# First group's third unit in seven products on summed factors, with three steps of ScalarE at other places

## The chip, the cores and the metric

The kernel runs on one core of one Trainium2 chip. The metric is device time in microseconds (us) of one execution; lower is better. TensorE (PE in the profile) multiplies matrices and writes to eight PSUM banks; VectorE (DVE) and ScalarE (ACT) do elementwise work and empty the banks; GpSimd (POOL) and SyncE (SP) here mostly issue DMAs. Each engine works through its own queue in order, and semaphores tie the queues together.

## The reference

A causal linear attention with decay, then a feed-forward layer:

```
for each block of 64 positions:                      # B=4, H=8, S=768, D=64
    intra = ((q_b @ k_b.T) * Dmask) @ v_b
    inter = (q_b * lam_pow) @ kv_state
    out   = intra + inter
    kv_state = lam_block * kv_state + (k_b * rev_pow).T @ v_b
x = out as (3072 tokens, 512)
h = x @ w_in                                         # 512 x 2048
g = h - tanh(h)
result = g @ w_out                                   # 2048 x 512
```

q, k, v and lam are float32. w_in and w_out come as 64-bit floats and are rounded to float32 on the chip.

## The kernel before, in words

**Groups and units.** The tokens are worked in NG = 6 groups of 512 (128 positions of each of 4 sequences). The 2048 columns of w_in are NU = 4 units of 512. A unit of h for one group is a 512 x 512 result, kept as a 2 x 2 grid of 256 x 256 corners named 11, 21, 12 and 22. A corner of h sits in one PSUM bank and goes through tanh (ScalarE) and a subtraction (VectorE) into the tiles g11, g21, g12, g22 (`hidden`, line 545).

**Two ways to a unit.** `up_plain` (line 953) computes a corner as a plain sum over four blocks of 128: 8 matmuls for each of 4 corners, 32 for a unit. `up` (line 540) computes one of seven products of Winograd's form of Strassen's scheme: sums of weight quarters (`ws`, made by `sums_in`, line 257) times sums of token quarters (`tt` and T3, made by `att_sums`, line 509), 4 matmuls for a product, 28 for a unit. Products are collected in three banks y, z and w: ScalarE copies y into w after product 1, so that product 2 adds to it; copies of y after products 6 and 7 and additions of z on VectorE give the other corners. `sums_in` overwrites the quarter a21 of the unit's weights with the sum S3, so that plain corners can't be computed from it any more. Before, group 0 uses `up_plain` for all its units; group 1 uses `up` for all.

**The stage in question** is group 0's: the weights of w_in are rounded while it computes (`round_block`, line 281: three ScalarE steps at lines 291 to 293 and two VectorE steps at 295 and 296 for each of 16 blocks of w_in and then 16 of w_out). Units 1 to 3 are done corner by corner, and between the corners lie pieces of the attention of group 1: `att_transpose`, `att_scores`, `att_state`, `att_inter`, `att_intra`, for sequences 0 and 1 (p0) and then 2 and 3 (p1). The list `turns` (line 1058) sets this order: unit, corner, how many blocks of w_out to round, attention pieces. Then follows the loop over kt (line 1080): `down_first` (line 984) multiplies 128 rows of g at a time with seven products, all seven accumulated in seven banks over kt = 0 to 7; `sums_out` (line 264) makes the weight sums of one kt and stores them to DRAM for later groups; kt = 2 and 5 keep their two blocks in `ws` tiles that are not yet used (`pair_tiles`, line 249). `sums_first` (line 979) makes S1 = g12 + g22 and g12 = g11 - g12 for one unit; `sums_late` the rest.

**Order.** The planner of the tile framework orders the instructions of each engine by the order in which they are written and by when it expects their inputs; what is ready may be pulled far forward. `tied(yes, op)` (line 125) keeps an instruction in the written order among the others that are tied on its engine. Between `att_inter` and `att_intra` (four banks left open) `held["yes"]` is true; `att_inter` ends in a small ScalarE read, `seen` (line 486), which the intra matmuls wait for. `att_state` (line 413) scales the old state on ScalarE (line 431); `powers` (line 108) fills `mask` on ScalarE and `fwd` on VectorE, both needed by group 1's attention. GI = 2 is the first group of the later, more finely split form.

Of the kernel before, what the change touches and what calls it, by code (L numbers as in the profile page):

```python
# [16 lines left out]
AL = mybir.AluOpType  # L17
# [7 lines left out]
def kernel(  # L25
# [223 lines left out]
    def pair_tiles(kt):  # L249

        if kt % 3 == 2:
            return tuple(ws[u].rearrange("p x k c -> p (x k) c")[:, 0:4] for u in (3, 2))
        wt = wst.tile([128, 8, 256], F32, name="wt", tag="w")
        return wt[:, 0:4], wt[:, 4:8]

# [156 lines left out]
    def att_state(g, bs):  # L412
        pair_ = slice(bs[0], bs[0] + 2)
        if g == 0:
            kv = bank("kv", "att", 4).rearrange("d (b p e) -> d b p e", b=2, p=NP)
            for n, b in enumerate(bs):
                kd, vn = raw[g, b]["k"], raw[g, b]["v"]
                for p in range(NP):
                    for j in range(2):
                        tc.keep_in_program_order(nc.tensor.matmul(  # L420
                            out=kv[ts(j, 64), n, p, :], lhsT=kd[:, 2 * p + j, :], rhs=vn[:, 2 * p + j, :],
                            start=n == 0 and p == 0, stop=True, skip_group_check=True))
            tc.keep_in_program_order(nc.scalar.activation(states(1)[0][:, pair_], kv, AF.Copy))
            return


        old, mid, new = (x[:, pair_] for x in states(g))
        subs = (0, 1) if g < NG - 1 else (0,)
        kv = [bank("kv", "att", 4).rearrange("d (b p e) -> d b p e", b=2, p=NP) for _ in subs]
        for p in range(NP):  # L430
            nc.scalar.activation(mid[:, :, p], old[:, :, p], AF.Copy, scale=fwd[:, p, HALF - 1:HALF])
        for n, b in enumerate(bs):
            kd, vn = raw[g, b]["k"], raw[g, b]["v"]
            for p in range(NP):
                for j in range(2):
                    for a in subs:
                        tied(g != GI, nc.tensor.matmul(
                            out=kv[a][ts(j, 64), n, p, :], lhsT=kd[ts(a, 64), 2 * p + j, :],
                            rhs=vn[ts(a, 64), 2 * p + j, :], start=n == 0 and p == 0, stop=True,
                            skip_group_check=True))  # L440
        nc.vector.tensor_tensor(mid, mid, kv[0], op=AL.add)
        for p in range(NP) if g < NG - 1 else ():
            nc.vector.scalar_tensor_tensor(out=new[:, :, p], in0=mid[:, :, p], scalar=fwd[:, p, HALF - 1:HALF],
                                           in1=kv[1][:, :, p], op0=AL.mult, op1=AL.add)
# [64 lines left out]
    def att_sums(g, bs):  # L509
        x0, x1 = xt[g, 0], xt[g, 1]  # L510
        b11, b21, b12, b22 = x0[:, 0:2], x0[:, 2:4], x1[:, 0:2], x1[:, 2:4]
        tt = xpool.tile([128, 3, 2, HB], F32, name="tt", tag="tt")
        nc.vector.tensor_tensor(tt[:, 0], b12, b11, op=AL.subtract)
        nc.vector.tensor_tensor(tt[:, 1], b22, tt[:, 0], op=AL.subtract)
        nc.vector.tensor_tensor(b12, b22, b12, op=AL.subtract)
        nc.vector.tensor_tensor(tt[:, 2], b21, tt[:, 1], op=AL.subtract)
        xt[g] = dict(B11=b11, B21=b21, B22=b22, T1=tt[:, 0], T2=tt[:, 1], T3=b12, T4=tt[:, 2])
# [27 lines left out]
    def up(g, u, n):  # L545
        a, bname = FACT[n]
        wt = {"A11": w1[u][:, 0:2, 0], "A12": w1[u][:, 2:4, 0], "S3": w1[u][:, 0:2, 1], "A22": w1[u][:, 2:4, 1],
              "S1": ws[u][:, 0], "S2": ws[u][:, 1], "S4": ws[u][:, 2]}[a]
        x = xt[g][bname] if bname != "B11" else xt[g, 0][:, 0:2]
        key = ("up", g, u)  # L550
        t, first = product_bank(key, n)
        for m in range(2):
            for kt in range(2):
                nc.tensor.matmul(out=t[:, m, :], lhsT=wt[:, kt, ts(m, 128)], rhs=x[:, kt, :],  # L554
                                 start=first and m == 0 and kt == 0, stop=kt == 1, skip_group_check=True)

        def dst(c):
            return hidden(g, c)[:, u]

        def finish(c, src):  # L560
            th = work.tile([128, 2, HB], F32, name="th", tag="th")
            nc.scalar.activation(th, src, AF.Tanh)
            nc.vector.tensor_tensor(dst(c), src, th, op=AL.subtract)

        y, z, w = (banks[key, x].rearrange("q (m c) -> q m c", m=2) if (key, x) in banks else None for x in "yzw")
        if n == 1:
            w = banks[key, "w"] = bank("w", "w", 1)
            nc.scalar.activation(w, banks[key, "y"], AF.Copy)
        elif n == 2:
            finish(11, w)  # L570
        elif n == 6:
            nc.scalar.activation(dst(12), y, AF.Copy)
        elif n == 7:
            nc.scalar.activation(dst(22), y, AF.Copy)
            nc.vector.tensor_tensor(dst(22), dst(22), z, op=AL.add)
            finish(22, dst(22))
        elif n == 4:
            finish(21, y)
        elif n == 3:
            nc.vector.tensor_tensor(dst(12), dst(12), z, op=AL.add)  # L580
# [355 lines left out]
    def every(steps):  # L936
        for _ in steps:
            pass
# [15 lines left out]
    def up_plain(u, cs):  # L954

        hm = {}
        for c in cs:
            a, t = divmod(c - 11, 10)
            hm[c] = bank("h", ("ya", "yb", "z", "w")[2 * t + a], 1).rearrange("q (m c) -> q m c", m=2)
        for i in range(KI):  # L960
            for c in cs:
                a, t = divmod(c - 11, 10)
                for m in range(2):
                    tied(u == 0 or held["yes"], nc.tensor.matmul(  # L964
                        out=hm[c][:, m, :], lhsT=w1[u][:, i, a, ts(m, 128)], rhs=xt[0, t][:, i, :],
                        start=m == 0 and i == 0, stop=i == KI - 1, skip_group_check=True))
                if (i, c) != (KI - 1, cs[-1]):
                    yield
        for c in cs:
            th = work.tile([128, 2, HB], F32, name="th", tag="th")  # L970
            nc.scalar.activation(th, hm[c], AF.Tanh)
            nc.vector.tensor_tensor(hidden(0, c)[:, u], hm[c], th, op=AL.subtract)  # L972
        yield
# [4 lines left out]

    def sums_first(u):
        g11, g12, g22, s1 = (hidden(0, c)[:, u] for c in (11, 12, 22, "S1"))  # L980
        nc.vector.tensor_tensor(s1, g12, g22, op=AL.add)
        nc.vector.tensor_tensor(g12, g11, g12, op=AL.subtract)

    def down_first(kt, ns):

# [39 lines left out]
    for b in (0, 1):  # L1025
# [29 lines left out]
    every(up_plain(0, (12, 22)))  # L1055
    sums_first(0)
    p0, p1 = attention(1)
    turns = [(1, 11, 2, ()), (1, 21, 2, ()), (1, 12, 2, ()), (1, 22, 2, ()), (2, 11, 0, ()), (2, 21, 1, p0[0:1]),
             (3, 11, 0, p0[1:3]), (3, 21, 1, p0[3:4]), (2, 12, 1, p0[4:]), (2, 22, 1, p1[0:1]), (3, 12, 1, p1[1:3]),
             (3, 22, 1, ())]  # L1060
    for u, c, n, more in turns:
        every(up_plain(u, (c,)))
        ahead = (u, c) == (2, 12)
        if ahead:
            run(more)
        weights(ready["done"] + n, u > 1)
        if not ahead:
            run(more)
        if c == 22:
            sums_first(u)  # L1070
            if u == 1:
                ready["to"] = len(blocks)
                load(B + 2)
                load_weights(NU * KI + 2)
                load(B + 3)
                load_weights(NU * KI + WAHEAD)
                load(2 * B)
                powers()
    sums_out(0)
    weights(NU * KI + 6, True)  # L1080
    for kt in range(KH):
        down_first(kt, (1, 2))
        if kt == 0:
            run(p1[3:4])
            down_first(kt, (5,))
            run(p1[4:])
        if kt + 1 < KH:
            sums_out(kt + 1)
        sums_late(kt)
        down_first(kt, (4, 7, 6, 3) if kt == 0 else (5, 4, 7, 6, 3) if kt + 1 < KH else (5, 6, 7, 4, 3))  # L1090
        if kt + 3 < KH:
            weights(ready["done"] + 2)
        if kt in (1, 4, 6):
            sums_in((1, 4, 6).index(kt))
    first_results()
    early.close()
    late["blk"] = ctx.enter_context(tc.tile_pool(name="blk", bufs=2 * B - 1))
# [174 lines left out]
```

## Time and profile before

| | us |
|---|---|
| three timed runs | 650.4, 649.97, 647.11 |
| their median | 649.97 |
| the profiled execution | 646.58 |
| its span | 644.8 |
| TensorE busy in the span | 635.1 |
| VectorE | 478.2 |
| ScalarE | 268.0 |

The span runs from the first to the last instruction of the program; the profiled execution's own time is 1.8 us more. TensorE's time as 'busy' counts each instruction from its start to a modelled end, and these overlap, so the step from one start to the next tells more than the length of one. A line of a timeline has the start, the length of a run of like instructions, the engine, the line of the kernel, what it writes and reads, the count, and the idle time of the engine before it with what released it.

### The profile page before, as it was taken

To read this page: it belongs to the slowest core of one execution; us is meant where nothing else is said; L and a number is where in the kernel's file an instruction comes from. 1 tells how busy PE (TensorE), PEld (TensorE's weight loads), DVE (VectorE), ACT (ScalarE), POOL (GpSimd) and SP (SyncE) were. 2 spreads that over 40 slices of the span, in tenths; PEclk is the share of its full clock that TensorE was granted. 3 is DMA by queue.
4 is the path that set the end of the run, shared out by engine and by line. 5 is a ranking of instruction groups with operands and counts; after the bars stand their busy time and mean duration, and the time that the engine had idled before them with its cause. 6 is when DMAs were issued, how large, how long until landed. Compare 5 with 4: busy or idle time off the path is not lost.

```text
span 644.8 us, 16628 instructions
## 1 busy us (share of the span) xinstructions
PE 635.1 (98%) x6440; PEld 583.6 (91%) x6440; DVE 478.2 (74%) x948; ACT 268.0 (42%) x620; POOL 229.0 (36%) x397
## 2 busy tenths in 40 slices
PE   8899999999999999999999999999999999999998
PEld 6788878888888999998999998999998899998997
DVE  4577597785888877579968579987668987467953
ACT  3799576503432422345331337233245332334310
POOL 0000355735443454411455430355321254521261
PEclk9999999999999999999999999999999999999999
DMA  9999988969765999884889976798883477732384
GB/s 216 233 244 232 294 265 268 348 187 267 210 164 126 288 278 298 224 188 112 230 236 304 280 203 157 184 276 249 253 198 80 138 234 241 248 105 77 100 296 145
DMA packets 166190, 139.80 MB, mean 217 GB/s; under 512 B 136864, under 2 KB 138016, under 8 KB 166112
## 3 DMA queue, kind: packets, MB, share of 16 engines
q0 software_dynamic: 31792, 104.62, 50.0%
q1 hardware_dynamic: 134176, 34.12, 25.9%
q8 instruction: 51, 0.84, 0.5%
q14 instruction: 27, 0.22, 0.1%
q10 hardware_dynamic: 144, 0.00, 0.0%
HBM read 111.94 MB, written 26.74 MB: 215 GB/s over the span
## 4 chain that ended last, share of the span: by engine, by line
PE 65%; issue 18%; POOL 8%; DVE 3%; DMA 3%; ACT 2%; SPq 2%; POOLq 0%; DVEq 0%
PE plain L849 10%; PE acc L993 7%; PE h L964 7%; PE y L906 6%; PE y L697 6%; PE zw L906 4%; PE y L554 4%; POOL wb L795 4%; PE z L697 3%; PE zs L619 2%; PE z L554 2%; PE y L619 2%; POOL wb L792 2%; PE op L501 1%; PE w L697 1%
## 5 line engine op out<-in xcount | busy, mean ns | idle before, releaser
L795 POOL DMA_DIRECT2D wb<-fine x133 | 71.8, 541 | 157.5 <-PE plain L849 107.8
L849 PE MATMUL plain<-wb,g 128*128 128x256 f32 x416 | 96.0, 381 | 0.0
L849 PEld LDWEIGHTS plain<-wb,g 128*128 128x128 f32 x416 | 77.5, 190 | 10.4
L964 PE MATMUL h<-xt,w 128*128 128x256 f32 x256 | 57.9, 382 | 1.8 <-DVE w L296 1.8
L798 POOL DMA_DIRECT2D wb<-factors x64 | 34.6, 541 | 69.2 <-PE z L697 47.9
L910 ACT ACTIVATE q<-y 128x128 f32<-128x128 f32 x76 | 21.1, 278 | 86.1 <-PE y L906 85.0
L964 PEld LDWEIGHTS h<-xt,w 128*128 128x128 f32 x256 | 47.7, 190 | 9.0 <-DVE w L296 2.0
L906 PE MATMUL y<-wb,g 128*128 128x128 f32 x336 | 44.8, 278 | 0.0
L792 POOL DMA_DIRECT2D wb<-fine_in x60 | 32.6, 545 | 29.3 <-PE z L697 11.0
L600 ACT ACTIVATE th<-g 128x512 f32<-128x512 f32 x48 | 29.5, 628 | 29.0 <-DVE g L625 28.9
L906 PEld LDWEIGHTS y<-wb,g 128*128 128x128 f32 x336 | 40.7, 192 | 0.7
L688 ACT ACTIVATE g<-y 128x512 f32<-128x512 f32 x24 | 14.3, 597 | 63.1 <-PE y L697 63.1
L404 ACT ACTIVATE k_nat<-k_nat,mask 128x64 f32<-128x64 f32 (+1 forms) x128 | 35.1, 338 | 0.6 <-DMA k_nat<-in_k_dram 0.6
L993 PE MATMUL acc<-wt,g 128*128 128x256 f32 x144 | 32.9, 380 | 0.2 <-DVE g L972 0.2
L601 DVE TENSOR_TENSOR g<-g,th 128x512 f32<-128x512 f32 x48 | 32.2, 687 | 0.4
L697 PE MATMUL z<-tt,wb 128*128 128x128 f32 x256 | 31.9, 275 | 0.0
L993 PEld LDWEIGHTS acc<-wt,g 128*128 128x128 f32 x144 | 27.2, 190 | 4.3 <-DVE g L972 0.6
L619 PE MATMUL y<-xt,w 128*128 128x256 f32 x128 | 30.3, 379 | 0.0
L619 PE MATMUL zs<-xt,ws 128*128 128x256 f32 x128 | 30.2, 379 | 0.0
L906 PE MATMUL zw<-wb,g 128*128 128x128 f32 x224 | 30.2, 278 | 0.0
L697 PEld LDWEIGHTS z<-tt,wb 128*128 128x128 f32 x256 | 30.2, 192 | 0.0
L292 ACT ACTIVATE r<-raw 128x512 int16<-128x512 uint32 x32 | 25.0, 782 | 8.3 <-DMA raw<-in_moe_w_out_dram 3.8
(236 smaller groups left out, 1476.2 us busy)
## 6 DMA issues: line engine op xcount, KB each, us to landing
wb<-fine POOLq DMA_DIRECT2D x133, 256.0 KB, 4.0
wb<-factors POOLq DMA_DIRECT2D x64, 256.0 KB, 4.3
wb<-fine_in POOLq DMA_DIRECT2D x60, 256.0 KB, 4.8
v_nat<-in_v_dram SPq DMA_DIRECT2D x24, 256.0 KB, 5.3
raw<-in_moe_w_out_dram POOLq DMA_DIRECT2D x12, 512.0 KB, 5.7
k_nat<-in_k_dram SPq DMA_DIRECT2D x20, 256.0 KB, 4.6
fine<-wt POOLq DMA_DIRECT2D x17, 256.0 KB, 3.4
raw<-in_moe_w_in_dram SPq DMA_DIRECT2D x8, 512.0 KB, 5.2
```

The costliest lines, as they stand in the source:

```text
L404: tc.keep_in_program_order(nc.scalar.activation(k_h, k_h, AF.Copy, scale=mask[0:rows, h % 2, h // 2, HALF - 1:HALF]))
L554: nc.tensor.matmul(out=t[:, m, :], lhsT=wt[:, kt, ts(m, 128)], rhs=x[:, kt, :], start=first and m == 0 and kt == 0, stop=kt == 1, skip_gro ...
L601: nc.vector.tensor_tensor(dst(c), src, th, op=AL.subtract)
L619: nc.tensor.matmul(out=t[:, m, :], lhsT=wt[:, kt, ts(m, 128)], rhs=x[:, kt, :], start=False, stop=kt == 1, skip_group_check=True)
L697: nc.tensor.matmul(out=dst[:, ts(u, 128)], lhsT=a, rhs=b, start=(x in (1, 5) or x == 2 and not filled) and u == 0, stop=True, skip_group_c ...
L792: nc.gpsimd.dma_start(out=t.rearrange("p m c -> p (m c)"), in_=fine_in[INNER.index(n_[1]), (5, 6, 3).index(x_)].rearrange("p u c -> p (u c)"))
L795: nc.gpsimd.dma_start(out=t.rearrange("p m c -> p (m c)"), in_=fine[TWICE.index(n_), SUB.index(x_)].rearrange("p u c -> p (u c)"))
L798: nc.gpsimd.dma_start(out=t, in_=factors[XAT[FACT[n_][1]]][:, 2 * x_:2 * x_ + 2, :])
L849: tied(held["yes"], nc.tensor.matmul(out=t[:, m, :], lhsT=a[:, u, kt, ts(m, 128)], rhs=wb[:, kt, :], start=first and u == 0 and m == 0 and ...
L906: tied(held["yes"], nc.tensor.matmul(out=dst, lhsT=a[:, u, :], rhs=wb[:, ts(u, 128)], start=x in (1, 2) and u == 0, stop=u == NU - 1, skip ...
L964: tied(u == 0 or held["yes"], nc.tensor.matmul(out=hm[c][:, m, :], lhsT=w1[u][:, i, a, ts(m, 128)], rhs=xt[0, t][:, i, :], start=m == 0 an ...
L993: tied(held["yes"], nc.tensor.matmul(out=acc[n][:, r, :], lhsT=a[:, ts(r, 128)], rhs=b, start=kt == 0 and r == 0, stop=kt == KH - 1, skip_ ...
```

## The change

Unit 2 of group 0 (its third) is computed by the seven products of `up` and no longer by `up_plain`. For this:

- `att_sums(0)` is written after unit 1's first corner. T3 goes into the place of S1 of unit 3, since group 0's B12 is still needed by unit 3's plain corners; `sums_first(3)`, which fills that place, moves to kt = 3.
- `sums_in(2)` moves from kt = 6 to after unit 1's second corner; `sums_in(1)` moves from kt = 4 to kt = 6; kt = 2 and 5 keep a block in `ws[1]` in place of `ws[2]`.
- `sums_first(1)` moves to kt = 0; both late ones are tied.
- unit 3's corners alternate between the banks w and yb.
- `powers` (mask) moves behind product 5 of unit 2.
- the sixth block of w_out is rounded behind the last intra matmuls; it and the two blocks after it are tied in kt = 0.
- the scaling of the state for group 2 is tied.

```diff
     def pair_tiles(kt):
-            return tuple(ws[u].rearrange("p x k c -> p (x k) c")[:, 0:4] for u in (3, 2))
+            return tuple(ws[u].rearrange("p x k c -> p (x k) c")[:, 0:4] for u in (3, 1))
...
         for p in range(NP):
-            nc.scalar.activation(mid[:, :, p], old[:, :, p], AF.Copy, scale=fwd[:, p, HALF - 1:HALF])
+            tied(g == GI, nc.scalar.activation(mid[:, :, p], old[:, :, p], AF.Copy, scale=fwd[:, p, HALF - 1:HALF]))
...
-        nc.vector.tensor_tensor(b12, b22, b12, op=AL.subtract)
+        t3 = b12 if g > 0 else hidden(0, "S1")[:, NU - 1]
+        nc.vector.tensor_tensor(t3, b22, b12, op=AL.subtract)
...
     def up(g, u, n):
-                nc.tensor.matmul(out=t[:, m, :], lhsT=wt[:, kt, ts(m, 128)], rhs=x[:, kt, :],
-                                 start=first and m == 0 and kt == 0, stop=kt == 1, skip_group_check=True)
+                tied(held["yes"], nc.tensor.matmul(
+                    out=t[:, m, :], lhsT=wt[:, kt, ts(m, 128)], rhs=x[:, kt, :], start=first and m == 0 and kt == 0,
+                    stop=kt == 1, skip_group_check=True))
...
     def up_plain(u, cs):
-            hm[c] = bank("h", ("ya", "yb", "z", "w")[2 * t + a], 1).rearrange("q (m c) -> q m c", m=2)
+            tag = ("w", "yb")[a] if u == NU - 1 else ("ya", "yb", "z", "w")[2 * t + a]
+            hm[c] = bank("h", tag, 1).rearrange("q (m c) -> q m c", m=2)
...
     def sums_first(u):
-        nc.vector.tensor_tensor(s1, g12, g22, op=AL.add)
-        nc.vector.tensor_tensor(g12, g11, g12, op=AL.subtract)
+        tied(u > 0, nc.vector.tensor_tensor(s1, g12, g22, op=AL.add))
+        tied(u > 0, nc.vector.tensor_tensor(g12, g11, g12, op=AL.subtract))
...
-    turns = [(1, 11, 2, ()), (1, 21, 2, ()), (1, 12, 2, ()), (1, 22, 2, ()), (2, 11, 0, ()), (2, 21, 1, p0[0:1]),
-             (3, 11, 0, p0[1:3]), (3, 21, 1, p0[3:4]), (2, 12, 1, p0[4:]), (2, 22, 1, p1[0:1]), (3, 12, 1, p1[1:3]),
-             (3, 22, 1, ())]
...
+    for c in (11, 21, 12, 22):
+        every(up_plain(1, (c,)))
+        weights(ready["done"] + 2)
+        if c == 11:
+            att_sums(0, None)
+        if c == 21:
+            sums_in(2)
...
+    turns = [(2, 1, 0, ()), (2, 5, 0, ()), (2, 2, 0, ()), (2, 6, 0, p0[0:1]), (3, 11, 0, p0[1:3]), (2, 7, 1, ()),
+             (3, 21, 0, p0[3:4]), (2, 4, 1, p0[4:]), (3, 12, 1, p1[0:1]), (2, 3, 1, p1[1:3]), (3, 22, 1, ())]
+    for u, x, n, more in turns:
+        if u == 2:
+            up(0, u, x)
+        else:
+            every(up_plain(u, (x,)))
+        ahead = (u, x) == (2, 4)
         if ahead:
             run(more)
-        weights(ready["done"] + n, u > 1)
+        weights(ready["done"] + n, True)
         if not ahead:
             run(more)
...
+        if (u, x) == (2, 5):
+            powers()
     sums_out(0)
-    weights(NU * KI + 6, True)
+    weights(NU * KI + 4, True)
     for kt in range(KH):
         down_first(kt, (1, 2))
         if kt == 0:
             run(p1[3:4])
             down_first(kt, (5,))
             run(p1[4:])
+            weights(NU * KI + 6, True)
...
         if kt + 3 < KH:
-            weights(ready["done"] + 2)
-        if kt in (1, 4, 6):
-            sums_in((1, 4, 6).index(kt))
+            weights(ready["done"] + 2, kt == 0)
+        if kt in (0, 3):
+            sums_first(1 if kt == 0 else NU - 1)
+        if kt in (1, 6):
+            sums_in(kt // 6)
```

More of the change, by code (lines that the diff above doesn't have):

```diff
@@ L514, in att_sums @@
         nc.vector.tensor_tensor(tt[:, 1], b22, tt[:, 0], op=AL.subtract)
-        nc.vector.tensor_tensor(b12, b22, b12, op=AL.subtract)
+        t3 = b12 if g > 0 else hidden(0, "S1")[:, NU - 1]
+        nc.vector.tensor_tensor(t3, b22, b12, op=AL.subtract)
         nc.vector.tensor_tensor(tt[:, 2], b21, tt[:, 1], op=AL.subtract)
-        xt[g] = dict(B11=b11, B21=b21, B22=b22, T1=tt[:, 0], T2=tt[:, 1], T3=b12, T4=tt[:, 2])
+        xt[g] = dict(B11=b11, B21=b21, B22=b22, T1=tt[:, 0], T2=tt[:, 1], T3=t3, T4=tt[:, 2])
     def attention(g):
@@ L1057 @@
     p0, p1 = attention(1)
-    turns = [(1, 11, 2, ()), (1, 21, 2, ()), (1, 12, 2, ()), (1, 22, 2, ()), (2, 11, 0, ()), (2, 21, 1, p0[0:1]),
-             (3, 11, 0, p0[1:3]), (3, 21, 1, p0[3:4]), (2, 12, 1, p0[4:]), (2, 22, 1, p1[0:1]), (3, 12, 1, p1[1:3]),
-             (3, 22, 1, ())]
-    for u, c, n, more in turns:
-        every(up_plain(u, (c,)))
-        ahead = (u, c) == (2, 12)
+    for c in (11, 21, 12, 22):
[5 more added lines that the diff above has]
+            sums_in(2)
+    ready["to"] = len(blocks)
+    load(B + 2)
+    load_weights(NU * KI + 2)
+    load(B + 3)
+    load_weights(NU * KI + WAHEAD)
+    load(2 * B)
+    turns = [(2, 1, 0, ()), (2, 5, 0, ()), (2, 2, 0, ()), (2, 6, 0, p0[0:1]), (3, 11, 0, p0[1:3]), (2, 7, 1, ()),
[6 more added lines that the diff above has]
+        ahead = (u, x) == (2, 4)
         if ahead:
             run(more)
-        weights(ready["done"] + n, u > 1)
+        weights(ready["done"] + n, True)
         if not ahead:
             run(more)
[L1069 to L1078, printed above, removed]
+        if (u, x) == (2, 5):
+            powers()
     sums_out(0)
-    weights(NU * KI + 6, True)
+    weights(NU * KI + 4, True)
     for kt in range(KH):
```

## The prediction

> **What bounds the kernel now.** I read the busy table first, then TensorE's busy time by stretches of 10 us over the first 200 us, then who TensorE waited for, then the timelines of TensorE and ScalarE over the stage that the diff touches (30 to 140 us), and last the timelines behind it.
>
> ```profile
> PE 635.1 (98%) x6440; PEld 583.6 (91%) x6440; DVE 478.2 (74%) x948; ACT 268.0 (42%) x620; POOL 229.0 (36%) x397
> ```
>
> TensorE is busy for 98% of the span, and the granted clock is full in all 40 slices. The list of TensorE's waits for 30 to 200 us has three entries only:
>
> ```profile
> PE op L501 <- ACT seen L486: 0.9, 1, 0.9
> PE h L964 <- DVE w L296: 0.8, 1, 0.8
> PE acc L993 <- DVE g L972: 0.2, 1, 0.2
> ```
>
> The second is the last wait of the start-up, at 30.22 us. So from there on a matmul less is worth its full step, and a new wait costs its full length, unless something later takes it back. The timeline of TensorE (start, length, line, idle time before it with its releaser) gives the step and the two waits:
>
> ```profile
> 30.22 29.62 PE L964 MATMUL h<-xt,w 128*128 128x256 f32 x136 [0.81 <-DVE w L296]
> 59.67 0.60 PE L340 MATMUL tp<-ident,q_nat 128*128 128x128 f32 x4
> ...
> 90.92 1.89 PE L993 MATMUL acc<-wt,g 128*128 128x256 f32 x8
> 93.00 1.13 PE L993 MATMUL acc<-wt,g 128*128 128x256 f32 x4 [0.19 <-DVE g L972]
> 94.06 1.16 PE L482 MATMUL op<-qd,state 64*64 64x64 f32 x64
> 95.15 1.13 PE L993 MATMUL acc<-wt,gS 128*128 128x256 f32 x4
> 97.15 1.16 PE L501 MATMUL op<-ss,v_nat 64*64 64x64 f32 x64 [0.88 <-ACT seen L486]
> ```
>
> 136 instructions take 59.67 - 30.22 = 29.45 us, 0.2165 us each (the 379 ns that the page gives is one instruction's length; they overlap). Each written matmul of this shape is two instructions: a unit has 4 corners x 4 x 2 = 32 matmuls, four units 128, and the page counts 256. The wait at 93.00 costs 93.00 - 90.92 - 8 x 0.2165 = 0.35 us. That at 97.15: 97.15 - 95.15 - 4 x 0.2165 = 1.13, less the 0.19 that the same switch cost in the first half (71.74 + 16 x 0.2165 = 75.20, next start 75.39): 0.94 us. What stood ahead of `seen` in ScalarE's order:
>
> ```profile
> 94.51 0.79 ACT L292 ACTIVATE r<-raw 128x512 int16<-128x512 uint32 x1 [0.95 <-DVE ws L296]
> 95.17 0.76 ACT L293 ACTIVATE r<-raw 128x512 f16<-128x512 f32 x1
> 95.80 1.25 ACT L431 ACTIVATE state<-state,fwd 128x128 f32<-128x128 f32 x4
> 96.95 0.15 ACT L486 ACTIVATE seen<-op 128x4 f32<-128x4 f32 x1
> ```
>
> `seen` reads what the inter matmuls (94.06 to 95.22) leave, and two rounding steps and four scalings of group 2's state (written far later, pulled forward by the planner since they were untied) run before it.
>
> **The change part by part.** Times are of this execution; unit 2 starts at 30.22 + 104 x 0.2165 = 52.74.
>
> *Products for corners.* 28 matmuls for 32 is 8 instructions less: 8 x 0.2165 = **-1.73 us**. [...]
>
> *Added VectorE work.* Group 0's token sums (L513 to L516: 4 of 0.69), two additions of z (2 x 0.685); moved up are unit 2's weight sums (4 x 0.683, from after 134 us to about 47), moved back is unit 1's pair at 54.32 and 55.27. Up to 60 us that is 2.7 + 2.7 - 1.4 = 4.0 us more; the stretches 30 to 60 leave VectorE 3.7 + 1.7 + 2.7 = 8.1 us idle. Unit 2's last block is rounded at 47.06 and S1 is wanted at 52.74 + 8 x 0.2165 = 54.47: 7.4 us of cover. Cost 0; without that cover up to the 4.0 us.
>
> *Added ScalarE work.* Three copies of 0.6 us. The critical one seeds bank w between product 1 (ends 54.47) and product 2 (starts 56.20). Here ScalarE is full:
>
> ```profile
> 53.46 0.67 ACT L291 ACTIVATE w<-raw 128x512 f32<-128x512 f32 x1
> 54.03 0.77 ACT L292 ACTIVATE r<-raw 128x512 int16<-128x512 uint32 x1
> 54.66 0.77 ACT L293 ACTIVATE r<-raw 128x512 f16<-128x512 f32 x1
> 55.29 1.68 ACT L111 ACTIVATE mask<-mask 64x256 f32<-64x256 f32 x4
> 57.00 0.60 ACT L971 ACTIVATE th<-h 128x512 f32<-128x512 f32 x1
> ```
>
> Behind the rounding the copy ends at 55.29 + 0.58 = 55.9 and TensorE loses nothing; behind the mask too, at 57.6, it loses 1.4. The mask is now written behind the copy, so I take 0.2, range 0 to 1.4.
>
> *Banks.* Unit 3's corner 11 wants bank w at 61.42; product 2 leaves it at 57.94, and tanh and subtraction need about 1.5 us (57.00 to 58.32 for another corner). Cover 1.9 us; behind the first six scalings of group 1's state (58.81 to 60.68) 0.6 would be lost. I take 0. Corner 22 of unit 3 moves from w to yb. Down-product 2, the one that waits at 93.00, then finds w long free, and yb is wanted only by product 6, behind two attention pieces: **-0.35**.
>
> *Second half's scores.* Today q and k are copied at 82.56 to 84.6, behind a rounding, and scores start at 85.33, a corner (16 instructions) after the transposes. Now one product (8 instructions) lies between, while as many as before (96) lie ahead of the transposes: scores are wanted at 85.33 - 1.73 = 83.6. Copies at their old place would cost 84.6 - 83.6 = 1.0; directly behind the transposes (4 steps of 0.48 from 80.6, as from 61.06 to 62.49) they are done by 82.7 and cost nothing. I take 0.3, range 0 to 1.0.
>
> *ScalarE ahead of `seen`.* Group 2's scaling is tied to its place in group 1's stage, where ScalarE is 22 to 48% busy (170 to 200 us) and its sum is not wanted before 204.45; the sixth block's rounding is written behind the intra matmuls. Ahead of `seen` remain only earlier blocks, the last of which ended at 87.9. **-0.94**, range 0 to -0.94: TensorE has only product 5 (0.87 us) between the two attention pieces, so one rounding step of 0.78 in the way gives most of it back. What the moves cost: the sixth block now runs from about 99.6 to 101.4 and its four differences end by 103.5, wanted at 108.71. Tied too, the next pair's rounding waits for its tile (102.00 today) and holds unit 1's pair of sums on VectorE to about 106.2, wanted at 108.71. Both free. The raw buffer of the sixth block comes free later, and POOL's queue holds the next raw load and the factor stores behind it; the last pair's differences end at 133.54 and are wanted at 138.93, 5.4 us of cover.
>
> *ws[1] for ws[2]*, and unit 1's weight sums from 129.7 to about 134: wanted after 155. Nothing. SP's loads keep their place.
>
> Sum: -1.73 - 0.35 - 0.94 + 0.2 + 0.3 = **-2.5 us**: the profiled execution's 646.58 (span 644.8) would be 644.1. That execution is faster than all three timed runs (median 649.97, 647.11 to 650.4). So I put the same difference on the median: **647.5**.
>
> **Rivals.**
> 1. *All of it, no new wait, and TensorE's one long wait near the end goes too* (0.59 us at 618.92, on a piece from DRAM): -1.73 - 0.35 - 0.94 - 0.59 = -3.6, 646.4. For it: every new wait has a place in ScalarE's order where it costs nothing. Against: that piece is requested when TensorE frees a buffer, so it should move along.
> 2. *New bank waits eat the gain.* Unit 2 and 3 now share four banks with ScalarE copies in the chain. [...] This change packs more onto w and yb. With the upper ends above, 1.4 + 0.6 + 1.0 = 3.0 against 1.73 + 0.35 + 0.94 = 3.0 saved: 650.0. Against: by the rows only the seed copy has less than a microsecond of cover.
> 3. *ScalarE's order becomes the bound, slower than before.* ScalarE is full from 30 to 55 us, and the planner orders what isn't tied. A block's rounding takes it 1.8 us (from 29.29 to 31.09). One block ahead of the seed copy (cover 0.3), of the second half's copies (0.9) and of `seen` (0.6) costs 1.5 + 0.9 + 1.2 = 3.6, with 1.73 + 0.35 = 2.1 saved, since `seen`'s 0.94 isn't: +1.5. Two blocks ahead of the first two and `seen` as it is: 3.3 + 2.7 - 2.1 = +3.9, 653.9. So it is slower from about one block at two of these places, and by more than 0.5% from two. For it: the copies stood behind a block today. Against: from 60 to 80 us ScalarE is free for 6.7 of 20 us, so a copy that is ready seldom has to queue.
> 4. *The products don't run as written*, because the planner moves untied matmuls: the count below would still fall by 8, so -1.73 stays and only the waits differ. It is part of the forecast's range and gets no chance of its own.
>
> **How the numbers follow.** Forecast 0.55, first rival 0.2, second 0.15, third 0.1. A measurement of this kernel can tell about 0.5% (3.2 us) from no change. The forecast (0.4%) and the second lie within it, the first just beyond, the third beyond on the other side; as the timed runs spread over 3.3 us, a little of the forecast goes beyond too: faster 0.25, same 0.65, slower 0.1. Range: from the profiled execution's level with all known gains, 646.58 - 3.0 = 643.5, to the second rival with some of the spread, 650.5.
>
> **What would show it.** Instructions at the plain corner's line 192 and at the product's line 280 (now 256 and 224). No wait of TensorE for `seen` and none for bank w at the first down-product. The seed copy ahead of the mask. The first down-product starting at 90.92 - 1.73 = 89.2, plus any new wait; group 1's first product at 143.24 - 2.5 = 140.7. I am wrong if TensorE shows a wait of over a microsecond between 52 and 90 us, or if that start moves and the span doesn't.

## The result, and the profile after

The changed kernel takes 650.86 us (median of 20 executions, 648.62 to 652.57), the kernel before 649.45 (20 executions, 646.04 to 652.70): a ratio of 1.0031, 95% interval 1.0017 to 1.0044. Forecast was a fall of 2.5 us; it is a rise, of 1.4 us by the two medians and of 2.0 by the ratio. The profiled execution took 650.84 us with a span of 649.1 (646.58 and 644.8 before).

The first part went as forecast. The page's busy table has eight matmul instructions less, 8 x 0.2165 = 1.73 us:

```profile
PE 636.7 (98%) x6432; PEld 583.6 (90%) x6432; DVE 481.6 (74%) x954; ACT 269.2 (41%) x623; POOL 228.7 (35%) x397
```

The list of TensorE's waits from 30 to 200 us (total, times, longest) has lost `seen` and bank w's `g L972`, and has two new entries:

```profile
PE acc L996 <- DVE g L1004: 3.1, 2, 2.7
PE h L967 <- DVE w L296: 1.2, 1, 1.2
PE sp L362 <- ACT kt L342: 0.3, 1, 0.3
```

TensorE's timeline shows where they stand. Both kernels start this stage at 30.22. The second half's scores wait a little (84.70), the first down-product starts at 89.81 (90.92 before), and the intra matmuls follow without a wait:

```profile
84.70 0.69 PE L362 MATMUL sp<-qt,kt 64*64 64x64 f32 x32 [0.28 <-ACT kt L342]
85.21 1.11 PE L437 MATMUL kv<-v_nat,k_nat 64*64 64x64 f32 x64
86.26 3.72 PE L967 MATMUL h<-xt,w 128*128 128x256 f32 x16
89.81 1.89 PE L996 MATMUL acc<-wt,g 128*128 128x256 f32 x8
...
126.07 1.60 PE L996 MATMUL acc<-wt,g 128*128 128x256 f32 x4 [2.75 <-DVE g L1004]
127.46 3.15 PE L996 MATMUL acc<-ws,g 128*128 128x256 f32 x8
130.45 1.03 PE L996 MATMUL acc<-ws,gS 128*128 128x256 f32 x4
```

kt = 1's product 5 starts at 100.56, against 102.67: 2.11 us gained. Then it is lost: 0.56 us at 104.57 and 2.91 at 126.07 on L1004, the second difference of `sums_late` (L1001 before), and 0.25 at 116.15 on L1003, the first. Behind the longest wait come 8 matmuls at twice their step, 1.7 us more. Group 1's first product starts at 146.85 instead of 143.24, 3.6 us later; behind it this profile loses only 0.7 us more to its end.

VectorE's timeline shows what held L1004 at 126. It is written behind the rounding of kt = 6's two blocks (L295, L296) and `sums_first(3)` (L984), and ran in that order:

```profile
119.04 0.43 DVE L1003 TENSOR_TENSOR g<-gS,g 128x256 f32<-128x256 f32 x1 [1.27 <-PE acc L996]
122.82 1.06 DVE L295 TENSOR_SCALAR wt<-wt 128x512 uint32<-128x512 uint32 x2 [3.35 <-ACT wt L291]
123.80 1.27 DVE L296 CUSTOM_DVE_ANT_0 wt<-wt,r 128x1024 uint16<-128x1024 uint16 x2
125.00 0.68 DVE L984 TENSOR_TENSOR gS<-g,g 128x512 f32<-128x512 f32 x1
125.60 0.41 DVE L1004 TENSOR_TENSOR g<-g,g 128x256 f32<-128x256 f32 x1
```

L1004's own input was there from 119.5 on. The 3.35 us before L295 come from ScalarE, which had a step of another block ahead of it, and that block (number 13, counted from 0) had not landed:

```profile
121.50 0.78 ACT L292 ACTIVATE r<-raw 128x512 int16<-128x512 uint32 x1 [6.58 <-DMA raw<-in_moe_w_out_dram]
122.14 1.22 ACT L291 ACTIVATE wt<-raw 128x512 f32<-128x512 f32 x2
```

It landed at 121.39; before, at 117.41. Its buffer was free at about 107.6, when ScalarE's last step on block 9 ended, but POOL's queue issued the load only at 113.38, behind seven stores of kt = 3's factors:

```profile
107.34 0.54 POOL L216 DMA_DIRECT2D raw<-in_moe_w_out_dram  x1 [1.93 <-ACT wt L291]
107.87 0.55 POOL L272 DMA_DIRECT2D factors<-wt  x1
...
113.38 1.10 POOL L216 DMA_DIRECT2D raw<-in_moe_w_out_dram  x2 [0.78 <-DMA factors<-wt]
```

POOL's timeline of the kernel before:

```profile
108.15 0.55 POOL L216 DMA_DIRECT2D raw<-in_moe_w_out_dram  x1 [0.59 <-ACT wt L291]
...
111.34 1.07 POOL L216 DMA_DIRECT2D raw<-in_moe_w_out_dram  x2
```

There block 13's load left 2.0 us sooner, although its buffer came free later (at 108.4): only four of the seven stores stood between it and block 12's load. The other half of the 4 us is the transfer itself: 8.0 us from issue to landing against 6.1. Why it took longer is not shown.

In the kernel before, L1001 of that kt ran at 121.93, between the two L296, and TensorE waited for nothing:

```profile
120.60 0.41 DVE L1000 TENSOR_TENSOR g<-gS,g 128x256 f32<-128x256 f32 x1
120.93 0.68 DVE L296 CUSTOM_DVE_ANT_0 wt<-wt,r 128x1024 uint16<-128x1024 uint16 x1
121.53 0.48 DVE L295 TENSOR_SCALAR wt<-wt 128x512 uint32<-128x512 uint32 x1
121.93 0.41 DVE L1001 TENSOR_TENSOR g<-g,g 128x256 f32<-128x256 f32 x1
122.26 0.68 DVE L296 CUSTOM_DVE_ANT_0 wt<-wt,r 128x1024 uint16<-128x1024 uint16 x1
```

(Of `tied` it was said that an instruction keeps its place among the tied ones. In these traces it runs right behind the one written just before it on its engine, tied or not: `sums_first(3)` behind block 13's L296 here, and behind kt = 3's L1004 in the first experiment.)

### The profile page after: what moved, and what is told of

The parts are those of the page before. It is cut to its first block, busy times and chain, and to the rows that moved or that the text cites. A ratio compares the mean times of both kernels' runs of the same rounds, so it can differ in the third digit from the quotient of the medians.

```text
span 649.1 us, 16621 instructions
## 1 busy us (share of the span) xinstructions
PE 636.7 (98%) x6432; PEld 583.6 (90%) x6432; DVE 481.6 (74%) x954; ACT 269.2 (41%) x623; POOL 228.7 (35%) x397
## 4 chain that ended last, share of the span: by engine, by line
PE 63%; issue 11%; POOL 5%; DMA 2%; DVE 0%; POOLq 0%
PE plain L851 12%; PE y L699 8%; PE y L908 7%; PE zw L908 5%; PE y L555 4%; PE z L699 4%; PE acc L996 3%; POOL wb L797 3%; PE y L621 3%; PE zs L621 3%; PE z L555 2%; PE w L699 2%; DMA wb<-fine 2%; PE sp L362 1%; PE op L482 1%
## 5 line engine op out<-in xcount | busy, mean ns | idle before, releaser
L967 PE MATMUL h<-xt,w 128*128 128x256 f32 x192 | 43.5, 382 | 1.8 <-DVE w L296 1.7
L967 PEld LDWEIGHTS h<-xt,w 128*128 128x128 f32 x192 | 35.8, 190 | 7.4 <-DVE w L296 2.0
L216 POOL DMA_DIRECT2D raw<-in_moe_w_out_dram x12 | 6.9, 574 | 85.8 <-ACT r L293 83.0
```

The costliest lines, as they stand in the source:

```text
L967: tied(u == 0 or held["yes"], nc.tensor.matmul(out=hm[c][:, m, :], lhsT=w1[u][:, i, a, ts(m, 128)], rhs=xt[0, t][:, i, :], start=m == 0 an ...
```

## The experiments

Ratios are to the kernel before in the same series, by medians, with 95% intervals. Theory A: VectorE's order at kt = 4 passes a late block on to TensorE. Theory B: the late blocks hold TensorE whatever VectorE's order. Theory C: the added VectorE work is too much. Theory D came up later.

**1. late_free.** The changed kernel; at kt = 4 the rounding comes behind the pair of differences. POOL's and ScalarE's order stay. (`sums_late` now returns its second difference. The diffs here show only the lines that matter.)

```diff
-            weights(ready["done"] + 2, kt == 0)
+            weights(ready["done"] + (0 if kt == 3 else 2), kt == 0)
+        if kt == 3:
+            load_weights(len(blocks))
...
-        sums_late(kt)
+        g21 = sums_late(kt)
+        if kt == 4:
+            with tc.issue_after(g21.ins):
+                weights(ready["done"] + 2)
```

> The changed kernel with one thing moved: in VectorE's order the g21 subtraction of kt = 4 stands ahead of the rounding of the 13th and 14th w_out blocks, and unit 3's sums ahead of both; ScalarE's and POOL's orders are the same as in the changed kernel. Theory A (the wait of 2.9 us at 126.07 comes from VectorE's order: the subtraction stands behind a rounding whose block lands at 121.4): the blocks land as late as before, but TensorE's wait and the 1.9 us of doubled steps behind it go, span about 649.1 - 4.8 = 644.3, ratio to before 0.996 to 0.999. Theory B (the late landing holds TensorE whatever VectorE's order): a wait of over 1.5 us stays between 117 and 140 us, ratio 1.001 or more. Theory C (the added VectorE work is too much for the stage): waits of similar sum appear in other places, ratio 1.002.

Measured 1.0025 (1.0006 to 1.0043). Its profile shows A right and the time shows it short: block 13 landed as late as 120.83, no wait at 126 is left, and group 1 starts at 141.95, 1.3 us ahead of the kernel before. Yet the median is not below. In the profile the lead is lost by 303 us: ScalarE waits 2.21 us for rows of k at 286.72 (theory D below), and TensorE stands still for 1.54 us at 302.81, in the middle of a run of 64 like matmuls and for nothing that the profile shows. What the first of these costs TensorE by itself is at most 0.2 us in this profile.

**2. before_back.** The kernel before, kt = 4's second difference queued behind the rounding of both blocks of kt = 6 (`pin` holds its last instruction).

```diff
-        nc.vector.tensor_tensor(g21, g21, g11, op=AL.subtract)
+        with tc.issue_after(pin["op"]) if kt == 4 else ExitStack():
+            nc.vector.tensor_tensor(g21, g21, g11, op=AL.subtract)
```

> The kernel before with the g21 subtraction of kt = 4 queued on VectorE behind the rounding of both blocks of kt = 6, as it stands in the changed kernel, and nothing else changed. Theory A: the subtraction then waits for the 14th block, which lands at 117.4 there; its rounding ends by 123.0 and TensorE wants the subtraction at about 124.3, so the order alone costs 0 to 0.5 us (ratio 0.999 to 1.002); only order and late landing together cost 2.9 us and more. If the order alone is the cause, a wait of 2 us or more shows at kt = 4 and the ratio is 1.004 to 1.008.

Measured 0.9997 (0.9978 to 1.0015): with blocks that land in time the order costs nothing.

**3. before_scalar_moves.** The kernel before with the moves on ScalarE and none of the products.

```diff
-(2, 21, 1, p0[0:1])
+(2, 21, 0, p0[0:1])
-            nc.scalar.activation(mid[:, :, p], old[:, :, p], AF.Copy, scale=fwd[:, p, HALF - 1:HALF])
+            tied(g == GI, nc.scalar.activation(mid[:, :, p], old[:, :, p], AF.Copy, scale=fwd[:, p, HALF - 1:HALF]))
...
-    weights(NU * KI + 6, True)
...
             run(p1[4:])
+            weights(NU * KI + 6, True)
...
-            weights(ready["done"] + 2)
+            weights(ready["done"] + 2, kt == 0)
```

> The kernel before with the ScalarE moves alone (first w_out block's rounding a corner later, sixth block behind the intra matmuls, kt = 0 tied, group 2's scaling tied); no products. POOL then issues the late loads in the same order as the changed kernel, while VectorE's order at kt = 4 stays that of before. Theory A: the late loads land as late as in the changed kernel (14th block at 120 to 122 us) but cost nothing; the wait for seen (0.94 us) goes: span about 643.9, ratio 0.997 to 1.000. Theory B: a wait of 2 us or more at kt = 3 to 5, ratio 1.003 to 1.007.

Measured 1.0059 (1.0040 to 1.0078), slower than the changed kernel: the moves alone cost about 4 us and the products are not to blame. Theory C falls. Only 1.15 us of it is a wait in the first group (at 117.73, on kt = 3's first difference, which stands behind the rounding of block 11); group 1 starts at 143.74, 0.5 us later than before. The rest is far behind, and ScalarE's timeline has it:

```profile
291.78 1.06 ACT L404 ACTIVATE k_nat<-k_nat,mask 128x64 f32<-128x64 f32 x4 [5.47 <-DMA k_nat<-in_k_dram]
```

The same line of the kernel before:

```profile
286.41 1.07 ACT L404 ACTIVATE k_nat<-k_nat,mask 128x64 f32<-128x64 f32 x4 [0.60 <-DMA k_nat<-in_k_dram]
```

This is the scaling of group 3's k rows, at the start of group 2. It holds the copies and tanhs queued behind it, and TensorE loses 4.6 us in six waits from 293 to 322 (the one at 306.86, of 0.66 us, on nothing that the profile shows). Hence **theory D**: SyncE's queue is a second path. Once the last block of w_out is through, it issues 128 loads of pieces of q and k of group 2 and 112 of group 3, and only then group 3's k rows. In the kernel before the first of these leaves at 129.86 and the rows' own load at 281.97, 0.63 us for each on average; the rows land at 286.39, and ScalarE wants them at 285.8.

**4. sp_loads.** The changed kernel, all raw loads of w_out on SyncE's queue.

```diff
-                load_block(nc.sync if by_sync else nc.gpsimd, raw64, *block, by_sync)
+                load_block(nc.sync, raw64, *block, by_sync)
```

> The changed kernel with all w_out loads issued from SyncE's queue, where no factor store stands ahead of them. Theory A and B: the 13th to 16th blocks land 3 us or more earlier, no wait at kt = 4, kernel at the level of the forecast: 649.1 - 5.5 = 643.6 span, ratio 0.995 to 0.998. Theory C: ratio stays at 1.002.

Measured 1.0061 (1.0038 to 1.0085), against what I expected. Block 13 landed at 116.77 and the wait at 126 went, but group 2's natural rows now stood behind the raw loads, the block loads started at 134.19, and ScalarE waited 5.41 us for the k rows. It fits D, which I had not formed then.

**5 to 8.** D's remedy, `nat`: from group 3 on, the natural rows (k and v as they lie in DRAM) of sequences 0 and 1, which the expectations call units, are queued behind 64 of the block loads. Its edit:

```diff
             for b in range(B - 1):
                 load_blocks(g, b, "qk")
+                if b == 1 and g > GB:
+                    load_natural(g, 0, nat)
+                    load_natural(g, 1, nat)
             load_blocks(g, 3, "q")
-            for b in (0, 1):
-                if b not in first:
-                    load_natural(g, b, nat)
```

`before_nat`, `after_nat` and `late_free_nat` have this edit on the kernel before, the changed kernel and late_free.

> The kernel before, with one edit of SyncE's queue: from group 3 on, the natural k and v rows of units 0 and 1 are loaded behind 64 of the group's 128 block loads, not behind 112 of them; nothing else differs. Theory D (new, from the traces of the first experiments): SyncE's queue of q and k block loads is a second path. It starts when the last w_out block is through, needs about 157 us from there to group 3's k rows, and ScalarE's scaling of these rows waits for it at 286 us, by 0.6 us in the fastest profile and by 5.4 us in the two slow ones. If so, this edit takes the wait away: the slow executions go and the median falls by 2 to 3 us, to a ratio of about 0.996. Theories A and B (all is decided in the first group): no change, 1.000 within 0.001.

Measured 1.0005 (0.9987 to 1.0023). D's guess for this kernel was wrong: its cover is short (0.6 us in the profile) but mostly enough.

> The changed kernel with the same edit of SyncE's queue. Theory D: it falls by as much as the kernel before does, from 1.003 to about 0.999 to 1.000, and what is left against the kernel before with this edit (about 3.5 us) is the first group's loss at kt=4. Theories A and B: 1.003, as the changed kernel.

Measured 1.0023 (1.0003 to 1.0042), from 645.05 to 651.36. The fastest of them is the profiled one (span 643.3): block 13 happened to land at 118.14, and TensorE did not wait at 126.

> The changed kernel with the weights of kt=6 queued behind kt=4's subtraction on VectorE (as in late_free, which starts group 1 by 2 us sooner than the kernel before and still measured 1.0025), and the edit of SyncE's queue. Theory D: late_free lost its 2 us to the load chain; without it the time is that of the kernel before with the edit, less 2 us: ratio about 0.993. Theories A and B alone: 1.0025, as late_free.

Measured **0.9976** (0.9960 to 0.9993), 645.23 to 647.88: now a gain shows, 1.6 us, though block 13 landed at 120.53. after_nat, of the same series, differs by late_free's edit of VectorE's order alone and is 3.1 us slower (medians 649.38 and 646.24): that is the price of the order, and B falls. D had the size of the gain over late_free about right (0.5%), not that of the whole (0.993).

**products_only** is the changed kernel with ScalarE's order as before:

```diff
-(2, 6, 0, p0[0:1])
+(2, 6, 1, p0[0:1])
-            tied(g == GI, nc.scalar.activation(mid[:, :, p], old[:, :, p], AF.Copy, scale=fwd[:, p, HALF - 1:HALF]))
+            nc.scalar.activation(mid[:, :, p], old[:, :, p], AF.Copy, scale=fwd[:, p, HALF - 1:HALF])
...
-    weights(NU * KI + 4, True)
+    weights(NU * KI + 6, True)
...
-            weights(NU * KI + 6, True)
...
-            weights(ready["done"] + 2, kt == 0)
+            weights(ready["done"] + 2)
```

> The seven products and all that they need, with ScalarE's order of the rounding as before: the sixth block ahead of the loop, kt=0's blocks and the state's scaling free, one more block rounded with the third unit's fourth product (one turn later than before). Theory B: the loads land as in the kernel before (block 13 at about 117 to 119), no wait over 1 us at kt=4, and the head gains what the products save, 2 us. Then with theory D: block loads start at about 130, the gain up to group 1 is met by the load chain in part of the executions: ratio 0.997 to 0.999. Theory A (VectorE's order of kt=4 is the cause, the loads are not): the wait at kt=4 stays at 2 to 3 us, 1.002 to 1.003.

Measured 1.0023 (1.0008 to 1.0038). Block 13 landed at 117.96 and nothing waits at 126, but TensorE gives all of it back and more (group 1 starts at 144.50) at `seen`, which stands behind a rounding in ScalarE's order:

```profile
97.55 1.16 PE L501 MATMUL op<-ss,v_nat 64*64 64x64 f32 x64 [2.92 <-ACT seen L486]
```

So the moves are needed: TensorE comes 2 us sooner and would only wait 2 us longer there.

**9. late_sums_nat.** late_free_nat, unit 1's pair of sums behind kt = 1's differences.

```diff
+        if kt == 1:
+            sums_first(1)
...
-        if kt in (0, 3):
-            sums_first(1 if kt == 0 else NU - 1)
+        if kt == 3:
+            sums_first(NU - 1)
```

> late_free_nat, with unit 1's pair of sums moved on VectorE from the end of kt=0 to behind kt=1's pair of differences. In late_free_nat's trace TensorE still waits 0.57 us at 104.99 for kt=1's second difference, which stands behind these sums (0.6 us each). If the rest of the gain is lost there, the wait goes and the ratio falls from 0.9976 to about 0.9968. Rival: the sums are then late for kt=2's products, or the time is decided elsewhere: 0.9976, no change.

Measured 0.9965 (0.9947 to 0.9982). The wait at 105 is gone; one of 0.63 us stands at 116.2.

**10. moves_nat.** before_scalar_moves with `nat`.

> The kernel before with the ScalarE moves alone (1.0059 by itself), and the natural rows loaded earlier in SyncE's queue. Theory D (the late rounding starts the block loads 3 us later, and ScalarE waits for the rows behind them): most of the loss goes, ratio about 1.001 to 1.002, with the wait of 1.1 us at 117.7 left. Theory B (the loss is in the first group): it stays at 1.005 to 1.006.

Measured 0.9988 (0.9969 to 1.0007), against 1.0059 without: within the noise, the moves' whole loss was the wait for the rows.

**11 and 12. chain_late and chain_late_nat** were to hold SyncE's chain in the kernel before.

```diff
+                with tc.issue_after(pin["op"].ins) if (g, b) == (GB, 0) else ExitStack():
+                    load_blocks(g, b, "qk")
```

> The kernel before, with the first of SyncE's block loads held until kt=6's second difference has run on VectorE, at about 134.4 us instead of 129.9: the chain starts 4.5 us later, and nothing of the first group changes. Theory D: with some 1 us of cover, TensorE loses about 3 us around 290: ratio 1.004 to 1.006. Rival (the block loads have cover, and the slow executions come from the first group): 1.000.

> chain_late, with the natural rows loaded earlier in SyncE's queue. Theory D: what waited at 286 no longer stands at the chain's end, so the late start costs nothing or only the few tenths of the wait at 226: ratio 1.000 to 1.001. Rival (a late start of the loads costs by contention, not by that wait): as chain_late, 1.004 to 1.006.

`pin` holds kt = 6's second difference; chain_late_nat has the edit `nat` too. Measured 0.9987 (0.9969 to 1.0006) and 0.9982 (0.9966 to 0.9998). They tell nothing of D, because the edit held nothing: the first block load left at 130.17. As before_nat and chain_late_nat then differ in nothing that the trace shows, 1.0005 and 0.9982 also say what the measurement is worth: some 0.2%.

**13 and 14. chain_longer and chain_longer_nat.** The kernel before with ten more loads in SyncE's chain.

```diff
                 load_blocks(g, b, "qk")
+                for x in range(10 if (g, b) == (GB, 0) else 0):
+                    blk = k[3, x % 8, ts(g, BLK), ts(x // 8, 32)]
+                    tc.keep_in_program_order(
+                        nc.sync.dma_start(out=spare[x], in_=blk.rearrange("(r t) a -> t r a", t=32)))
```

> The kernel before with SyncE's chain made longer by itself: behind the first 32 block loads ten more reads of the same form (one quarter of a block each, into a spare piece of DRAM that nothing uses). The first group is untouched. By the chain's own pace (0.5 to 0.63 us for one load) everything behind them comes 5 to 6 us later, group 3's k rows too. Theory D: with some 1 to 2 us of cover, TensorE loses 3 to 4 us at about 290: ratio 1.005 to 1.007. Rival (the block loads are covered and the losses come from the first group): 1.000.

> chain_longer, and the natural rows of units 0 and 1 loaded behind 64 of the block loads from group 3 on. Theory D: the rows are in time again, 1.000 to 1.001. Rival (the ten reads cost by the traffic that they add, not by the wait at the chain's end): as chain_longer.

Measured 1.0049 (1.0028 to 1.0069) and 0.9991 (0.9970 to 1.0013). This is D's proof, for the kernel before: the first group is untouched (group 1 starts at 143.66), the chain alone is longer, and the same wait comes and goes with the rows' place. ScalarE's timeline of chain_longer, then of chain_longer_nat:

```profile
292.36 1.06 ACT L409 ACTIVATE k_nat<-k_nat,mask 128x64 f32<-128x64 f32 x4 [5.29 <-DMA k_nat<-in_k_dram]
```

```profile
286.20 1.05 ACT L409 ACTIVATE k_nat<-k_nat,mask 128x64 f32<-128x64 f32 x4
```

and TensorE's waits of chain_longer from 200 to 400 us. All but the last stand behind that ScalarE wait, from 294 to 308; the last, at 226.29, waits for nothing that the profile shows. The list of chain_longer_nat is empty:

```profile
PE zs L624 <- DVE zs L615: 1.8, 2, 1.1
PE plain L854 <- ACT plain L843: 0.7, 1, 0.7
PE y L624 <- ACT y L614: 0.7, 1, 0.7
PE kv L442 <- issue: 0.5, 1, 0.5
```

**15. after_again.** The changed kernel for a second profile.

> The changed kernel once more, for a second profile: in the first one block 13 landed at 121.4 and TensorE waited 2.9 us at 126.1; in after_nat, whose first group is the same, it landed at 118.1 and TensorE did not wait. Theory A with D (two losses, each in part of the executions, either of which hides the gain): ratio 1.002 to 1.004; if the block lands by about 119 there is no wait at 126, and ScalarE waits 2 us or more for group 3's k rows at about 286 instead; if it lands at 121 or later, the wait at 126 is there. Rival (one loss, always the same): the wait at 126 is there wherever the block lands.

Measured 1.0045 (1.0023 to 1.0066). Another execution, another place: block 13 landed at 120.24, the wait at 125 is 0.30 us, one of 1.01 stands at 117.70 on kt = 3's L1003, behind the rounding of block 11 (landed at 113.23, 111.57 in the first profile), group 1 starts at 144.10, and ScalarE's line at the k rows now reads

```profile
289.47 1.06 ACT L404 ACTIVATE k_nat<-k_nat,mask 128x64 f32<-128x64 f32 x4 [2.57 <-DMA k_nat<-in_k_dram]
```

with 1.6 us lost by TensorE at 300 to 305, most of it in a stop of 0.85 us at 304.86 for nothing that the profile shows. In the first profile, where TensorE came 2.7 us later, ScalarE waited 0.54 us for the rows and TensorE lost nothing. So a late TensorE hides the late rows; that each loss stands in for the other in full is not shown.

**16. late_sums_again.** late_sums_nat beside the changed kernel.

> late_sums_nat once more, beside the changed kernel on one chip: if both losses are away, 0.9965 within 0.0015, and some 3.5 to 4.5 us less than the changed kernel. If the first measurement was chance, 0.999 to 1.000.

Measured 0.9993 (0.9971 to 1.0016), less good than the first time (0.9965); the two intervals only just meet. Its profiled execution was the slowest of twelve, with 1.7 us lost at 327, for nothing that the profile shows, and 2.3 us at 367 on VectorE's L688. VectorE had stood still for 7.49 us until 363.47, until the last pieces of k in SyncE's queue had landed (363.09). Two other profiles with `nat`, late_sums_nat and chain_longer_nat, have the same wait of VectorE (4.25 and 5.04 us, with no wait of TensorE behind it), and no profile without `nat` has it, though the edit leaves the place of these pieces in the queue. Why they come late in these three is open. Against the changed kernel of the same series it is 4.1 us faster (646.94 and 651.00). So the version clearly beats the changed kernel. That it beats the kernel before is likely, by 0.1 to 0.35%, and late_free_nat's 0.9976 agrees.

## Why the prediction was wrong

- *Products, -1.73.* Right: 8 instructions less, and the counts 192 and 280 at the two lines.
- *Bank w, -0.35, and `seen`, -0.94.* Right, both waits are gone.
- *Added VectorE work, 0.* Right: TensorE waits for none of unit 2's products.
- *Seed copy, 0.2.* It ran at 55.49, ahead of the mask at 56.04, and cost nothing.
- *Second half's copies, 0.3.* 0.58 us: they stayed at 82.60 to 84.6, behind a rounding, by the gap of 0.09 and 0.49 at the scores. About 0.3 more at 92.16, in the inter matmuls, was in no term.
- Up to kt = 1 that makes 2.1 us for 2.5, and the first down-product 89.81 for 89.2. The sum was sound as far as it reached.
- **The step that failed** is the one that costed the late rounding: "The raw buffer of the sixth block comes free later, and POOL's queue holds the next raw load and the factor stores behind it; the last pair's differences end at 133.54 and are wanted at 138.93, 5.4 us of cover", after "Both free". It named the right queue and then took the cover from one consumer of the last pair. The pair before it was late, and the one that paid was no consumer: kt = 4's difference, which only stands behind that pair's rounding in VectorE's queue. Before, it was done at 121.93 + 0.41 = 122.34 and wanted at 124.26 (kt = 4's last product, 12 matmuls behind the 121.66 of TensorE's timeline): 1.9 us of cover, not 5.4, against a block that landed 4 us later. Nor was it the buffer that came late: block 9's was free at 107.6 (108.4 before), and half of the 4 us was POOL's order, half the longer transfer.
- **"SP's loads keep their place"** was true of the order and was the second miss: nothing behind 140 us was priced for SyncE's queue. SyncE's block loads start when the last block of w_out is through, and their end was waited for by 0.60 us in the profile before. The nine profiles with the moves and this queue issue the seventh of these block loads at 135.1 to 136.6, the eight without at 133.2 to 134.5, while group 1 starts up to 1.3 us sooner (late_free). The first block load is no later in most of them (129.3 in late_free, 129.9 before). What exactly delays that stretch (the last block's landing, or the other transfers of that time: the DMA share from 130 to 134.2 us was 0.97 in the changed kernel, 0.76 before) is not shown.
- *The form of the sum.* With two limits in parallel, terms don't add. late_free (one loss gone) 1.0025, after_nat (the other gone) 1.0023, both gone 0.9976. What reached kt = 1, less the 0.57 us at 104.99 that late_free_nat still has, is 2.11 - 0.57 = 1.5 us, and late_free_nat gained 1.6 (0.0024 x 647.5); so close an agreement is partly luck, as a ratio repeats to some 0.2%, 1.3 us.
- *Rivals.* The third had the right sign, but put the place at the copies and `seen`, in ScalarE's order; the loss came at 126, in VectorE's. That its +1.5 us is near the measured rise is luck. "I am wrong if TensorE shows a wait of over a microsecond between 52 and 90" named too short a stretch; of "if that start moves and the span doesn't" the half came true: the first down-product moved ahead to 89.81, and the span grew.

That the wait at 126 comes in only part of the executions is read from three profiles with this order (landing at 121.39, 120.24 and 118.14: 2.9, 0.3 and 0 us; the load had left at 113.38, 115.11 and 113.42, so it is mostly the transfer that varies). How often, no run tells. How much of the changed kernel's loss D makes is known from medians alone: late_free 1.0025 and late_free_nat 0.9976, each against its own series. In the profiles of the changed kernel and of late_free, what TensorE loses behind the late rows is at most 0.5 us (300.26 in after_again), beside the stops that no view explains.

## What to carry to other kernels

When a step is moved later, follow what it frees (a buffer, then the load behind it in its queue) to the next instruction that stands behind that load's consumer on every engine, and take the cover of the nearest of them, not of the last. Before adding up gains, look for a chain that runs beside the changed stage and is waited for much later by tenths of a microsecond: its end is the ceiling, and a DMA queue in which a few wanted rows stand behind a hundred loads not yet wanted is a likely one. Taking one of two such limits away can show nothing; take both. Then look at the next consumer of the same queue.

## What the runs showed of the hardware

TensorE's granted clock fell behind two of its waits and not behind a third. The changed kernel's windows (from, to, length, busy time and count of PE, PEld, DVE, ACT, POOL, then the granted clock, the DMA share and GB/s) have, behind 2.75 us of idle time at 126.07:

```profile
124.00:126.00 2.00, 0.00 (x0) 0.00 (x0) 2.00 (x5) 1.42 (x3) 1.80 (x4) 1.00 0.85 324
126.00:128.00 2.00, 1.93 (x6) 1.61 (x7) 1.97 (x6) 0.29 (x1) 1.66 (x3) 0.65 0.98 318
128.00:130.00 2.00, 2.00 (x6) 1.58 (x5) 1.32 (x4) 2.00 (x4) 2.00 (x4) 0.50 0.90 268
130.00:132.00 2.00, 2.00 (x11) 1.75 (x10) 2.00 (x5) 0.22 (x1) 1.62 (x3) 1.00 0.97 322
```

In windows of 0.2 us the clock is 1.00 up to 126.4, 0.50 from 126.6 to 130.0 and 1.00 again from there: some 3.4 us at half (the 0.65 of the second window above is 1.4 us of them). That costs 1.7 us on top of the wait of 2.9 (the 12 matmuls from 126.07 to 130.45 took 4.38 us, at their usual step 12 x 0.2165 = 2.60): that wait cost 1.6 times its length. late_sums_again shows it behind 2.24 us at 367.54 (0.69, 0.50 and 0.96 in the windows of 2 us from 368 to 374); products_only doesn't behind 2.92 us at 97.55 (1.00 in those from 96 to 102, mean clock 1.000). So the length of the wait did not tell by itself: the clock fell behind 2.24 and 2.75 us and not behind 2.92. What else decided is not shown.

TensorE also stood still inside a run of like matmuls, for nothing that the profile shows as waited for: 1.54 us at 302.81 in late_free, 0.85 us at 304.86 in after_again, 0.66 us at 306.86 in before_scalar_moves, 0.5 us at 226.29 in chain_longer, and on L437 0.4 us in late_free_nat and, between 285 and 312 us, in sp_loads. The profiles of the kernel before and of the changed kernel have none of 0.2 us or more from 30 to 650 us. ScalarE waited over 2 us for the rows in five profiles; four of them (late_free, after_again, before_scalar_moves, sp_loads) have such a stop behind that wait, and chain_longer has none there. What ties the two is not shown.
